# Attention then a mixture of experts on one core: smaller first row transfers, first v rows in float32, a later start of GpSimd's queue and a scripted opening

## The chip, the cores and the metric

The kernel runs on one core of one Trainium2 chip. The metric is the device time of one execution in microseconds; the number before the change is the median of three runs, 360.63 us (360.43 to 360.79). A core has five engines that run on their own and meet through semaphores: TensorE (PE, matrix products and transposes), VectorE (DVE), ScalarE (ACT), GpSimd (POOL) and SyncE (SP). Transfers between the large memory and the core's own memory are issued by an engine's queue: here by SP and ACT (plain copies and transposes) and by POOL (copies that also change float32 into bfloat16). All are carried out by the same 16 DMA engines.

## What is computed

Attention with a sliding window of 128 rows and 4 sink rows, over 4 batches of 8 heads of 768 rows of 64, and then a mixture of 4 experts over the 3072 rows of 512 that come out of it:

```python
scores = scale * q @ k.T                      # per batch and head
keep = (pos[None, :] < 4) | ((rel >= 0) & (rel < 128))
a = softmax(where(keep, scores, -1e9))
x = concat_heads(a @ v)                       # 3072 x 512
p = domain_probs / (domain_probs.sum(-1) + 1e-9)
out = sum over e of p[:, e] * (relu(x @ w1[e]) @ w2[e])   # w1: 512 x 1024, w2: 1024 x 512
```

Everything that comes in and goes out is float32; the products are done in bfloat16.

## The kernel before

**Tiles and stages.** A batch has three groups g of 256 rows, and its heads come in four pairs hp of two heads (2 x 64 = 128 columns). For batch 0 a pair of a group goes through five steps. "flip" (`transposes`) turns q and k rows on TensorE into qkT. "todo" is `scores`: the products sps, and exponentials on ScalarE into aT. For group 0 of batch 0 the mask is added beforehand as a product of ident with the tile low (L698); else VectorE multiplies by mask0 or mask1. "values" forms od from aT and vx (a tile of v rows with a column of ones), and divides by that column: reciprocal R and a product on VectorE into onat. "turn" transposes onat into xT on TensorE, copied out by ScalarE or VectorE. For groups 1 and 2 there are sink terms too: `sink_keys` and `sink_values`, computed on GpSimd for batch 0 from the rows vsf.

**Experts.** `Mixture` takes xT through the first layer (hps, L1098, into H) and the second (acc, L1425) for the first two groups of batch 0; w1 and w2 are an expert's weights. The other groups, and for some experts the first two also, use a scheme with seven half-size products (cps, L1181; acc, L1350) in place of eight, which needs sums of weight blocks ("forms", L402 to L408 and L367 to L373) and of xT blocks (token differences T, made by `tokens`, L1150), all on VectorE.

**What sets the order.** The program is straight-line code written out by a planner that runs while the kernel is built. It keeps an estimated clock per engine in the dictionary t ("sw" is GpSimd's transfer stream, "hw" the other), calls `later` to put off work of VectorE and ScalarE with a time from which it is ready and a slack, and in a loop at the end picks the next step of TensorE among those that are ready: attention (`Attention.options`), first-layer units, second-layer products. Constants such as TOKEN0, GATE0, MARGIN, GROW or STEP0 are its slacks, thresholds and priorities. While nothing is ready early in the run it puts in dummy products (`idle_products`, L572), and it starts with nine of them.

**The opening.** `load_first` (L285) loads the first 256 q and k rows of batch 0 in float32 as two halves of four heads: q on the sync queue, k on ScalarE's queue, 256 KB each. `cast_first` (L306) turns a half into bfloat16, q on VectorE and k on ScalarE. The sync queue then loads the routing table dp (L455), eight strips of sink rows vsf (L500) and the probabilities pr (L503). GpSimd's queue loads, in this order (L519 to L529): v 0 and 1, the rows tb 2 and 3 (q and k of group 1), v 2, the first quarter of w1 of expert 0, v 3, the other three quarters, w2 of expert 0. Later loads follow from the list `loads` (L1464). The gate rows (`gates_by_row`, L459) are normalised and stored once the planner's clock is past GROW.

Of the kernel before, what the change touches and what calls it, by code (L numbers as in the profile page):

```python
# [16 lines left out]
def kernel(  # L17
# [42 lines left out]
    NGATE = 5  # L60
    START = {0: (1, 0), 1: (0, 1), 2: (0, 0), 3: (0, 0)}
# [9 lines left out]
    EARLY = 0.138  # L71
    GATE = 5742
    GATE0 = 5043
    FORM = 19230
    FORM2 = 38137
    TOKEN0 = 220
# [4 lines left out]
    MARGIN = 828  # L81
    FULL = 8
    STEP0 = 0.155
    READY = 39
# [7 lines left out]
    GROW = 22996  # L92
# [16 lines left out]
    FLIP = 179  # L109
# [175 lines left out]
    def load_first():  # L285

        raw = {name: mo.tile([P, 2, 4, 2 * D], FP32, name=f"{name}raw", tag=f"wide{i}", bufs=1) for i, name in enumerate("qk")}
        for half in range(2):
            hs = slice(4 * half, 4 * half + 4)
            for name, src in (("q", q), ("k", k)):  # L290
                x = raw[name][:, half]
                (nc.sync if name == "q" else nc.scalar).dma_start(
                    out=x, in_=src[0, hs, 0:G, :].rearrange("h (p t) d -> p h (t d)", t=2),
                )
                nat[0, half, name, "raw"] = x
            landed["first", half] = ((4870.0, 5180.0), (7550.0, 7350.0))[half]
            t["sp"] += 530

# [7 lines left out]
    def cast_first(half):  # L306
        hs = slice(4 * half, 4 * half + 4)

        def cast(at):
            cast_at[half] = at  # L310

        part = join(2, cast)
        for i, name in enumerate("qk"):
            def run(engine, i=i, name=name):
                copy(
                    engine, first[name][:, :, hs, :],
                    nat[0, half, name, "raw"].rearrange("p h (t d) -> p t h d", t=2),
                )
                part(clock(engine, 512))
            later(("dve", "act")[i], landed["first", half][i], 0, run)  # L320
# [126 lines left out]
    load_first()  # L447
# [88 lines left out]
    low = [lent[:, 5 * P:8 * P], lent[:, 8 * P:10 * P]]  # L536
    nc.vector.tensor_scalar(
        out=low[0].rearrange("p (n q) -> p n q", n=3)[:, 0::2], in0=two, scalar1=LOW, scalar2=-LOW, op0=ALU.mult, op1=ALU.add,
    )
    nc.vector.tensor_scalar(out=low[0][:, P:2 * P], in0=own, scalar1=-LOW, scalar2=None, op0=ALU.mult)  # L540
    nc.vector.memset(low[0][0:NSINK, 0:2 * P], 0.0)
# [4 lines left out]
    t["dve"] = t["act"] = 4600.0  # L546
    cast_first(0)
    flush(4700.0)
    for x in vx:
        nc.vector.memset(x[:, :, D:DX], 1.0)  # L550
    t["dve"] += 240.0
# [5 lines left out]
    nc.vector.memset(half, 0.0)  # L557
    for ph in range(2):
        nc.vector.memset(half[64 * ph:64 * ph + 64, ph:ph + 1], 1.0)
    for x in ksd:  # L560
        nc.vector.memset(x, 0.0)
    for x, y in zip((mask0, mask1), low):
        nc.vector.tensor_scalar(out=x, in0=y, scalar1=1 / LOW, scalar2=1.0, op0=ALU.mult, op1=ALU.add)
    t["dve"] += 400.0
    cast_first(1)
# [13 lines left out]
    def transposes(b, g, hp):  # L579
# [3 lines left out]
        ready = max(cast_at[hp // 2] if (b, g) == (0, 0) else rows_at(b, g), free_at(2 if (b, g) == (0, 0) else 1))  # L583
        slots, trs = [], []
        for i in range(2 if (b, g) == (0, 0) else 1):
            slots.append(pick())
            trs.append(bank(slots[i], [P, 2, 2, P], BF16, "tr"))
            ring[slots[i]] = 1e12
        hs = slice(2 * hp, 2 * hp + 2)
# [17 lines left out]
        if (b, g) == (0, 0):  # L607
            part = join(2, copied)
            for i, engine in enumerate(("dve", "act")):
# [75 lines left out]
    def scores(b, hp, g, more=False):  # L685
# [10 lines left out]
        if biased:  # L696
            for ph in range(2):
                nc.tensor.matmul(sps[ph][:, 0:w], lhsT=ident, rhs=low[min(g, 1)], start=True, stop=False, skip_group_check=True)  # L698
# [62 lines left out]
    def values(b, hp, g):  # L761
# [47 lines left out]
        def run(engine):  # L809
# [3 lines left out]
            if b < ONACT:  # L813
# [47 lines left out]
    class Attention:  # L861
# [24 lines left out]
        def flip_ready(self):  # L886
            _, b, g, hp = self.flips[0]
            rows = cast_at.get(hp // 2, 1e12) if (b, g) == (0, 0) else rows_at(b, g)
            return max(rows, free_at(2 if (b, g) == (0, 0) else 1), scored_at.get(b - 1, 0.0))

        def options(self):

# [72 lines left out]
    class Mixture:  # L965
# [164 lines left out]
        def tokens(self):  # L1130
# [9 lines left out]
            if at > t["pe"]:  # L1140
                return
# [314 lines left out]
    idle_products(acc[1], 9)  # L1456
# [140 lines left out]
```

## Time and profile before

| | |
|---|---|
| median of three runs | 360.63 us (360.43 to 360.79) |
| profiled execution | 360.94 us |
| its span | 359.2 us |
| PE busy | 349.9 us (97%), 4678 matrix instructions |
| DVE busy | 309.0 us (86%), 703 instructions |
| ACT busy | 168.6 us (47%), 430 instructions |
| POOL busy | 68.9 us (19%), 90 instructions |
| q0, transfers of GpSimd's queue | 17.31 MB, 53.3% of 16 engines' span |
| q1, transfers of the sync queue | 19.32 MB, 29.9% |
| q10, transfers of ScalarE's queue | 0.52 MB, 0.6% |

The span goes from the first to the last event that the profiler shows; what the profiled execution took beyond it lies around it. In a line of the time line the columns are start, duration (both us), engine, line of the kernel, operation, tiles, shapes, number of instructions merged, and in brackets the idle time of the engine before it and what ended that. PEld is a weight load of TensorE; SPq, ACTq are issues of those queues. In the line of forty digits each digit is the busy share, in tenths, of a fortieth of the span (9.0 us). A matrix instruction's duration includes its way through the array, so instructions that follow each other overlap, and the pace of a group of them is the better measure.

### The profile page before, as it was taken

The numbers are of one execution on the slowest core, as the hardware profiler recorded it, in microseconds if no ns is written. First come the engines' busy times: TensorE is split into PE (matmuls) and PEld (weight loads), VectorE is DVE, ScalarE is ACT, GpSimd is POOL, SyncE is SP. The second block draws the span as 40 slices with busy tenths as digits, with TensorE's granted clock in tenths as the row PEclk, the third lists the DMA queues.
The fourth block names the chain that finished last, engine by engine and source line by source line (L and its number), as shares of the span: only waits on it lengthen the run. The fifth ranks groups of instructions, "written<-read, shape, count | busy, mean of one in ns | idle before, by whom it ended". The sixth has DMA issues, their size and how long they took to land.

```text
span 359.2 us, 11107 instructions
## 1 busy us (share of the span) xinstructions
PE 349.9 (97%) x4678; PEld 302.7 (84%) x4678; DVE 309.0 (86%) x703; ACT 168.6 (47%) x430; POOL 68.9 (19%) x90
## 2 busy tenths in 40 slices
PE   8899999999999999999999999999999999999995
PEld 3575687777588998998998998899899999999884
DVE  6779889998799799899699799799789899989630
ACT  5856341437883824556444732943752722222110
POOL 8934115211270531020030530000000000000000
PEclk9999999999999999999999999999999999999999
DMA  9999999999994999675077999131042211100011
GB/s 176 186 194 204 222 212 174 145 125 150 202 151 53 151 174 131 75 98 67 31 62 119 151 133 158 47 71 32 20 66 58 59 44 64 31 31 31 1 60 59
DMA packets 115318, 37.86 MB, mean 105 GB/s; under 512 B 97196, under 2 KB 110764, under 8 KB 115268
## 3 DMA queue, kind: packets, MB, share of 16 engines
q0 software_dynamic: 74416, 17.31, 53.3%
q1 hardware_dynamic: 39796, 19.32, 29.9%
q8 instruction: 36, 0.59, 0.7%
q10 hardware_dynamic: 1056, 0.52, 0.6%
q14 instruction: 14, 0.11, 0.1%
HBM read 41.03 MB, written 6.34 MB: 132 GB/s over the span
## 4 chain that ended last, share of the span: by engine, by line
PE 86%; DMA 6%; ACT 3%; DVE 2%; issue 1%; POOL 1%; SPq 0%; ACTq 0%; DVEq 0%
PE cps L1181 38%; PE acc L1350 34%; PE acc L1425 6%; DMA vx<-in_v_dram 3%; PE sps L704 2%; PE od L784 2%; PE hps L1098 2%; DMA kraw<-in_k_dram 2%; DMA scratch<-in_moe_domain_probs_dram 1%; ACT onat L823 1%; ACT aT L744 1%; PE od L777 1%; DVE aT L752 0%; DVE onat L814 0%; DVE osb L1435 0%
## 5 line engine op out<-in xcount | busy, mean ns | idle before, releaser
L1181 PEld LDWEIGHTS <-w 128*128 128x128 bf16 x1408 | 86.3, 98 | 3.2 <-issue 0.8
L1350 PEld LDWEIGHTS <-H 128*128 128x128 bf16 x720 | 66.4, 98 | 8.0 <-issue 1.6
L1215 DVE SCALAR_TENSOR_TENSOR H<-cps,gates 128x512 bf16<-128x512 f32 x105 | 69.6, 684 | 0.0
L1350 PE MATMUL acc<-w,H 128*128 128x256 bf16 x432 | 57.5, 273 | 0.5 <-ACT acc L1379 0.5
L1181 PE MATMUL cps<-T,w 128*128 128x128 bf16 x704 | 52.5, 219 | 0.5 <-DVE cps L1231 0.5
L1181 PE MATMUL cps<-xT,w 128*128 128x128 bf16 x704 | 52.0, 219 | 0.0
L744 ACT ACTIVATE aT<-sps 128x512 bf16<-128x512 f32 (+1 forms) x96 | 46.3, 573 | 3.5 <-PE sps L704 3.4
L1224 ACT COPY cps<-cps 128x512 f32<-128x512 f32 x44 | 25.4, 586 | 46.1 <-PE cps L1181 36.8
L1397 ACT COPY osb<-acc 128x256 f32<-128x256 f32 x40 | 15.2, 379 | 56.9 <-PE acc L1350 49.2
L823 ACT ACTIVATE onat<-od,R 128x64 bf16<-128x64 f32 x144 | 33.1, 352 | 17.8 <-DVE R L811 17.8
L1350 PE MATMUL acc<-wf,H 128*128 128x256 bf16 x288 | 39.2, 273 | 0.0
L1181 PEld LDWEIGHTS <-qkn 128*128 128x128 bf16 x576 | 35.1, 98 | 1.3
L1231 DVE TENSOR_TENSOR cps<-H,cps 128x512 f32<-128x512 f32 x40 | 27.7, 692 | 8.9 <-PE cps L1181 5.3
L1350 PEld LDWEIGHTS <-S 128*128 128x128 bf16 x320 | 30.2, 98 | 4.8 <-issue 1.4
L329 POOL DMA_DIRECT2D vx<-in_v_dram x24 | 21.4, 902 | 62.2 <-PE od L784 50.5
L1237 ACT COPY H<-cps 128x512 f32<-128x512 f32 x40 | 23.4, 593 | 19.3 <-PE cps L1181 19.2
L1425 PE MATMUL acc<-w,H 128*128 128x512 bf16 x128 | 30.1, 379 | 0.0
L1181 PEld LDWEIGHTS <-vf 128*128 128x128 bf16 x480 | 28.6, 98 | 0.3
L1246 DVE TENSOR_TENSOR H<-H,cps 128x512 f32<-128x512 f32 x40 | 27.0, 681 | 0.8 <-PE cps L1181 0.7
L1181 PE MATMUL cps<-T,qkn 128*128 128x128 bf16 x384 | 27.1, 219 | 0.0
L725 DVE TENSOR_TENSOR aT<-aT,mask 128x1024 bf16<-128x1024 bf16 (+1 forms) x36 | 23.1, 641 | 2.4 <-ACT aT L744 2.4
L1215 DVE SCALAR_TENSOR_TENSOR H<-H,gates 128x512 bf16<-128x512 f32 x35 | 23.9, 685 | 0.0
(125 smaller groups left out, 517.9 us busy)
## 6 DMA issues: line engine op xcount, KB each, us to landing
w<-in_moe_w_dram POOLq DMA_DIRECT2D x7, 1024.0 KB, 22.7
out_dram<-osb SPq DMA_DIRECT2D x23, 256.0 KB
gates<-gate_rows SPq DMA_DIRECT2D x40, 128.0 KB
vx<-in_v_dram POOLq DMA_DIRECT2D x24, 128.0 KB, 7.5
rows<-in_q_dram POOLq DMA_DIRECT2D x18, 128.0 KB, 7.0
rows<-in_k_dram POOLq DMA_DIRECT2D x18, 128.0 KB, 7.5
w<-in_moe_w_dram POOLq DMA_DIRECT2D x4, 256.0 KB, 8.8
kraw<-in_k_dram ACTq DMA_DIRECT2D x2, 256.0 KB
```

The costliest lines, as they stand in the source:

```text
L329: nc.gpsimd.dma_start(out=vx[tb][:, :, 0:D], in_=v[b, :, tb * P:(tb + 1) * P, :].rearrange("h p d -> p h d"),)
L725: nc.vector.tensor_mul(x, x, m[:, None, :].to_broadcast([P, n, 2 * w // n]))
L744: nc.scalar.activation(out=a[:, ph], in_=sps[ph][:, 0:w], func=AF.Exp, scale=scale)
L823: nc.scalar.mul(o[:, qi, hp, ph * D:(ph + 1) * D], od[:, qi, ph, 0:D], R[:, qi, ph])
L1181: nc.tensor.matmul(y[:, f], lhsT=A[:, d, f * P:(f + 1) * P], rhs=T[:, d], start=(m in ("P1", "P5") and f == 0 and d == 0), stop=(d == 1), ...
L1215: nc.vector.scalar_tensor_tensor(out=dst, in0=src, scalar=0.0, in1=gate, op0=ALU.max, op1=ALU.mult)
L1224: nc.scalar.copy(out=tiles["Y"], in_=y)
L1231: nc.vector.tensor_add(tiles["V"], c5, tiles["X"])
L1237: nc.scalar.copy(out=c5, in_=y)
L1246: nc.vector.tensor_add(c5, c5, y)
L1350: nc.tensor.matmul(x, lhsT=self.operand(b, g, e, m)[:, f], rhs=forms[e][m][:, f], start=(k == 0 and f == 0 and m in (("P1", "P5", "P2") if ...
L1425: nc.tensor.matmul(op, lhsT=H[:, fb // QF, fb % QF, s], rhs=w2_sb[e][:, fb, :], start=(fb == 0), stop=(fb == NFB - 1),)
```

## The change

- The first q and k rows come as four transfers each (one per head pair, 128 KB), k on ScalarE's queue, q on the sync queue, and are cast pair by pair; which engine casts and copies is set by the tuples KCAST and COPY0.
- v 0 and v 1 of batch 0 are loaded in float32 by the sync queue, behind q and ahead of the routing table, and cast by VectorE.
- GpSimd's queue starts with a copy of two elements of the third pair's raw k rows (HOLD0 = 3), and then loads in the order ORDER0: rows 2 and 3, two quarters of w1 of expert 0, v 2, v 3, the other two quarters, and w2.
- The first 16 attention steps of batch 0 follow SCRIPT0 (F flip, S scores, V values, T turn).
- The masks and clears of small tiles are put off on VectorE with a slack; the second mask tile low[1] and its two ScalarE activations go, and mask1 is made from own.
- In group 0 of batch 0 the pairs 1 and 3 are scaled on ScalarE (SCALE0).
- Token differences are not made before the planner's clock is at 28000 (TOKEN00), gate rows not before 30000 (GROW).
- Five dummy products at the start in place of nine (NIDLE), and other values for EARLY, GATE0, TOKEN0, MARGIN, STEP0, READY and FLIP.

```diff
+    SCRIPT0 = "FFSSFFSSVVTVTTTV"
+    FIRST = (3950.0, 4950.0, 5950.0, 6900.0)
+    KCAST = ("act", "act", "act", "dve")
+    COPY0 = (('any', 'act'), ('dve', 'act'), ('any', 'any'), ('dve', 'any'))
+    SCALE0 = (0, 1, 0, 1)
+    NTR = 2
+    NACT = 4
+    FIRSTV = (7300.0, 8600.0)
+    HOLD0 = 3
+    NIDLE = 5
+    CLEAR = 3000
+    ORDER0 = (10, 11, 0, 1, 6, 7, 2, 3)
-    EARLY = 0.138
+    EARLY = 0.109
-    GATE0 = 5043
+    GATE0 = 400
-    TOKEN0 = 220
+    TOKEN00 = 28000
+    TOKEN0 = 2000
-    MARGIN = 828
+    MARGIN = 2000
-    STEP0 = 0.155
-    READY = 39
+    STEP0 = 0.215
+    READY = 100
-    GROW = 22996
+    GROW = 30000
-    FLIP = 179
+    FLIP = 400
...
     def load_first():
-        raw = {name: mo.tile([P, 2, 4, 2 * D], FP32, name=f"{name}raw", tag=f"wide{i}", bufs=1) for i, name in enumerate("qk")}
-        for half in range(2):
-            hs = slice(4 * half, 4 * half + 4)
+        raw = {name: mo.tile([P, H, 2 * D], FP32, name=f"{name}raw", tag=f"wide{i}", bufs=1) for i, name in enumerate("qk")}
+        vraw = mo.tile([P, 2, H, D], FP32, name="vraw", tag="osb", bufs=1)
+        for hp in range(NHP):
+            hs = slice(2 * hp, 2 * hp + 2)
             for name, src in (("q", q), ("k", k)):
-                x = raw[name][:, half]
-                (nc.sync if name == "q" else nc.scalar).dma_start(
+                x = raw[name][:, hs]
+                (nc.scalar if name == "k" and hp < NACT else nc.sync).dma_start(
                     out=x, in_=src[0, hs, 0:G, :].rearrange("h (p t) d -> p h (t d)", t=2),
                 )
...
+        for tb in range(2):
+            nc.sync.dma_start(out=vraw[:, tb], in_=v[0, :, tb * P:(tb + 1) * P, :].rearrange("h p d -> p h d"))
+            t["sp"] += 530
+        return vraw
...
-    load_v(0, (0, 1))
-    t["sw"] += 500
-    for tb in (2, 3):
-        load_nat(0, tb)
-    load_v(0, (2,))
-    load_w1(0, 4, [0])
-    load_v(0, (3,))
-    for i in range(1, 4):
-        load_w1(0, 4, [i])
+    if HOLD0:
+        nc.gpsimd.tensor_copy(out=held, in_=raw[HOLD0 - 1])
+        t["pool"], t["sw"] = FIRST[(HOLD0 - 1)] + 300.0, 8000.0
+    for x in ORDER0:
+        if x < 4:
+            load_w1(0, 4, [x])
+        elif x < 8:
+            load_v(0, (x - 4,))
+        else:
+            load_nat(0, x - 8)
...
-    nc.scalar.activation(out=low[1][:, 0:P], in_=own, func=AF.Copy, scale=-LOW)
-    nc.scalar.activation(out=low[1][:, P:2 * P], in_=own, func=AF.Copy, scale=LOW, bias=-LOW)
...
+    for tb in range(2):
+        def cast_v(engine, tb=tb):
+            copy(engine, vx[tb][:, :, 0:D], vraw[:, tb])
+            landed["v", 0, tb] = clock(engine, 512)
+        later("dve", FIRSTV[tb], 200, cast_v)
...
-            if b < ONACT:
+            if b < ONACT and not (g == 0 and SCALE0[hp]):
...
         def options(self):
+
+            if not self.b and self.steps < len(SCRIPT0):
+                step = {"F": "flip", "S": "todo", "V": "values", "T": "turn"}[SCRIPT0[self.steps]]
+                mine = [x for x in self.choices() if x[1] == step]
+                if mine:
+                    yield from mine
+                    return
+            yield from self.choices()
...
-            if at > t["pe"]:
+            if at > t["pe"] or t["pe"] < TOKEN00:
                 return
...
-    idle_products(acc[1], 9)
+    idle_products(acc[1], NIDLE)
```

More of the change, by code (lines that the diff above doesn't have):

```diff
@@ L316, in run @@
                     engine, first[name][:, :, hs, :],
-                    nat[0, half, name, "raw"].rearrange("p h (t d) -> p t h d", t=2),
+                    nat[0, hp, name, "raw"].rearrange("p h (t d) -> p t h d", t=2),
                 )
-                part(clock(engine, 512))
-            later(("dve", "act")[i], landed["first", half][i], 0, run)
+                part(clock(engine, 256))
+            later(("dve", KCAST[hp])[i], landed["first", hp][i], 0, run)
     def rows_at(b, g):
@@ L445 @@
     forms_at = {}
-    load_first()
+    vraw = load_first()
+    raw = [nat[0, hp, "k", "raw"][:, 0, 0:2] for hp in range(NHP)]
     NT = Ntok // P
@@ L588, in transposes @@
             ring[slots[i]] = 1e12
+        trs = (trs * 2)[:2]
         hs = slice(2 * hp, 2 * hp + 2)
@@ L608, in transposes @@
             part = join(2, copied)
-            for i, engine in enumerate(("dve", "act")):
+            for i, engine in enumerate(COPY0[hp]):
                 def run(engine, i=i):
```

60 lines of the change are left out of this document (33 added, 27 removed).

## The prediction

> **What bounds the kernel now.** I read the page first, then the time line and the table of windows of the first 47 us, then the waits of the sync queue and the transfers by window.
>
> ```profile
> span 359.2 us, 11107 instructions
> PE   8899999999999999999999999999999999999995
> DMA  9999999999994999675077999131042211100011
> PE 86%; DMA 6%; ACT 3%; DVE 2%; issue 1%; POOL 1%; SPq 0%; ACTq 0%; DVEq 0%
> ```
>
> TensorE bounds it, and the DMA engines are full for the first 13 slices (117 us) as well. "Busy" flatters TensorE, since it counts dummy products and pipelining; so I count real work by its pace: 8 products of L1181 take 0.447 us, 4 of L1350 take 0.437, 8 of L1425 1.73, 8 of L1098 0.87. By that count the real work of the first 26.7 us is about 14.4 us and 12.3 are lost; from 26.7 to 47 about 1.3 of 20.3 are lost, and from 47 to 355.5 about 7 of 308. The change works where the 12.3 are.
>
> ```profile
> 2.28 1.95 POOL L329 DMA_DIRECT2D vx<-in_v_dram  x2
> 4.94 0.62 ACT L300 CAST qkn<-kraw 128x512 bf16<-128x512 f32 x1 [1.19 <-DMA kraw<-in_k_dram]
> 5.41 0.71 PE L593 MATMUL tr<-ident,qkn 128*128 128x128 bf16 x8
> 11.39 0.87 ACT L744 ACTIVATE aT<-sps 128x384 bf16<-128x384 f32 x2 [0.33 <-PE sps L704]
> 13.88 0.38 ACT L300 COPY xT<-tx 128x256 bf16<-128x256 bf16 x1
> 15.04 1.05 PE L1098 MATMUL hps<-xT,w 128*128 128x256 bf16 x8
> 16.81 0.27 PE L665 MATMUL sinks<-qkT,ksd 128*32 128x256 bf16 x1 [0.39 <-DVE qkT L300]
> 25.52 0.90 POOL L352 DMA_DIRECT2D w<-in_moe_w_dram  x1 [5.04 <-DMA w<-in_moe_w_dram]
> 26.70 1.90 PE L1425 MATMUL acc<-w,H 128*128 128x512 bf16 x8
> ```
>
> The reader is to see a chain: first real product at 5.41, last xT of group 0 at 14.26, first expert product at 15.04, first second-layer product at 26.70. The line at 25.52 dates w2 of expert 0: GpSimd was released by its landing, near 25. Two things set the pace: a chain through ScalarE and VectorE until some 23 us, and the software queue's stream of weights.
>
> ```profile
> SPq L500 <- DMA kraw<-in_k_dram: 3.0, 2, 1.5
> q10 hardware_dynamic: 440, 0.22, 92.4%
> q1 hardware_dynamic: 104, 0.06, 25.1%
> q0 software_dynamic: 66, 0.01, 13.2%
> ```
>
> The three queue lines are of 5 to 6 us: q0, GpSimd's queue, begins only as the first rows drain, though GpSimd issued at 2.28. Between 6 and 8 it moves 0.29 MB, which is the two v tiles. The sync engine stood twice for 1.5 us, each time until k rows landed: after q, k, q, k, the routing table and three sink rows, eight transfers, the next one waited.
>
> **Smaller first transfers.** The rows move at 0.33 and 0.32 MB/us (3 to 5 us). The first half pair is 0.52 MB, its k cast starts at 4.94; a pair's q and k are 0.26 MB, so 0.8 us less: 4.1. ScalarE now issues four transfers at 0.5 us (end 2.9), then the table load (1.28), so it is free at 4.2. A cast of half the columns is bounded by 0.31 and 0.62; I take 0.35. Transposes then start near 4.7, 0.7 sooner. The last rows still land near 7.0, as now (second k cast 7.03): bytes and pace are the same.
>
> **The fixed order** puts all four scores ahead of the values. ScalarE's work for group 0: three casts (1.05), some four copies (0.38 each, 1.5), eight exponentials (two in 0.87, 3.5), in all 6.1 from 4.2, with 0.3 for gaps 10.6, against 12.26 now. From there to the last xT it is 2.0 us now; pair 3 is scaled on ScalarE (four of L823 at 0.205, 0.82, against 0.42), so 13.0 against 14.26: **1.3 gained**. If each step waits for the other engines as now, only the 0.7 stays; bounds 0.7 and 1.7. The two mask activations that fall away (0.6) were hidden under the wait for k; so were the nine dummy products of which four go.
>
> That last edit could leave the array cold. The dummies start 0.43 us apart and only after 4.26 does the spacing fall to 0.15 or less, while the PEclk row says full speed throughout. The Trainium skill (TensorE: Matmul & The Clock Gate, Part 1) says that the array runs at half rate until a window of about 3.4 us was busy; the spacing agrees, about 2.9 us after the start at 1.40. The planner still fills waits above 220 ns with short dummies, so I charge nothing; cold, the 16 transposes and 8 bias products of group 0 would cost 16 x 0.055 + 8 x 0.16 = 2.2 us, mostly beside ScalarE.
>
> **v on the sync queue.** v 0 is the ninth transfer and waits for the first rows (4.1), then v follows the rows at once: 0.52 MB in 1.6 to 1.9 us, data 6.0 to 7.9, landed near 8.8 with the 0.9 that k takes from its last packets (6.0) to its cast (7.03). Two casts of 512 columns on VectorE (0.70 to 0.87 each) end by 9.6; the first values now wait for v until 9.30 anyway and come later in the new order. VectorE has 2.1 idle us of 6 between 4 and 10, which hides the 1.6. Routing table, sink rows and probabilities are behind v on the sync queue and slip some 2 us; sink values are read at 13.81, the rest after 22: hidden, with 3 us in hand for the sink rows.
>
> **GpSimd's queue.** It waits for the third k rows (6.1) and a tiny copy; first issue near 6.35. What is behind that wait: all later software loads, and the sink keys (13.17 now). From first issue to first packet it was 3.4 us at the start (2.28 to 5.7) and 1.5 later (142.79 to 144.3). First packets thus at 7.85 to 9.75; today the same stream, q and k rows of group 1, comes after v, at 8.0. The stream is moved by -0.15 to +1.75. I take **+0.6**, since the slow start overlapped with rows draining until 6. The skill (DMA: Bandwidth & Descriptors, Latency and other measured facts) gives about 1 us to the first byte of this path; by it the stream would open at 7.35, under v's tail, and the sum would be 0.6 better. The order inside it changes less: w1's first part comes after two loads rather than five, landing near 13.3 instead of 14.5, and v 2 and 3 (needed at 18.5) near 16.6. Two of GpSimd's issues (0.98 each) go.
>
> **VectorE's work moved.** Eight token differences (0.28 each, 2.3) leave 14.2 to 24.9 and the gate rows (1.05) leave 22.8, all to 28 us and later. That takes away the 0.39 at L665 and some 0.7 us around it, which keeps the gain above alive through group 1. But between 28 and 45 VectorE is busy 15.0 of 17 us, and between 47 and 84 36.2 of 37:
>
> ```profile
> 28.00:30.00 2.00, 2.00 (x33) 1.48 (x33) 1.97 (x4) 0.49 (x1) 1.76 (x2) 1.00 1.40 201
> 55.00:60.00 5.00, 5.00 (x36) 3.34 (x35) 5.00 (x9) 0.00 (x0) 1.75 (x3) 1.00 2.14 165
> ```
>
> (Third column from the sum on is VectorE.) 3.35 into 2.0 of room leaves 1.35 over. If VectorE runs ahead with the start, none is paid; I take 0.4 of 0 to 1.35. Other planner constants (margin, bias of choices, a slack of L1128) reorder later work; the waits of TensorE at 84 to 104 are 1.5 us, so I bound this by -1.5 and +1.5 and take 0.
>
> **Sum.** w2 of expert 0 lands at 25.5. By then TensorE can have done all that is done at 26.70 plus the product group that ran at 28.44 (0.87): lead 1.2 + 0.7 (of 0.87) = **1.9**, bounds 0.85 (stream at +1.75) and 2.8 (stream early, chain end 24.75). Less 0.4 for w2 of expert 1, 0.6 later than now when TensorE comes 1.5 early, less 0.4 for VectorE: **1.1**. The profiled execution took 360.94 us (span 359.2 and 1.7 around it), so 359.8; the median of the runs shown is 0.3 lower: 360.63 - 1.1 = **359.5**.
>
> **Rivals.** (a) The lead is real and hidden. Work that needs no expert 2 ends at 60.1; expert 2's forms run at 53.9 to 58.9 and hang on weights that landed near 47.6. If stream and forms slip 0.6 and VectorE gives nothing, TensorE waits there, and the end is where it was: **360.6**. For it: DMA full; against: 1.2 us between forms and use. (b) VectorE becomes the bound, the slower side: the 1.35 left over and 0.3 of late stream push forms and evictions after 47, and the lead is used up: no lead, plus 1.0 to 1.35, **361.7**. It decides once VectorE is without idle time from 28 to 47 and token differences still wait at 40. For it: its 98% from 47 to 84, and TensorE's 0.50 wait for L1231 at 85.6; against: VectorE gets the lead too. (c) All goes well: stream at 7.85, lead 2.8 kept, part of the 1.5 us at 84 to 104 closed: **357.6**. (d) It doesn't do what it says: rows still land in one bunch at 5 and group 0 ends near 14; that is in (a).
>
> **Chances.** Forecast 0.41 (own range 358.6 to 360.2), (a) 0.17, (b) 0.27, (c) 0.15. A measurement of this kernel tells 0.2% (0.72 us) from no change. Faster: (c) and most of the forecast, 0.50; same 0.21; slower 0.29. The range takes in (c) and (b) but for their tails: 357.2 to 362.0.
>
> **What would show it.** First L593 near 4.7; last xT near 13; first software packets between 7.9 and 9.7; first L1425 near 25.6; VectorE's windows 28 to 47; whether the distance between the two kernels at L1425's last product (95.4 now) is that at 26. If first software packets come after 9.7, or group 0 ends no sooner than 14, or the lead at 26 is gone at 95, I am wrong in that step.

## The result and the profile after

The changed kernel takes 362.52 us (median of 4 runs, 362.02 to 363.12), the kernel before 360.61 beside it: a ratio of 1.0051 with an interval of 1.0039 to 1.0063. It is slower by 1.9 us where 1.1 less was forecast. The profiled execution took 362.14 us, with a span of 360.4. It is a quick one of its kernel, and that of the kernel before (360.94) a slower one, so the two traces are 1.2 us apart and show two thirds of the loss.

The page of the kernel after: its first line, the rows of the slices for TensorE and the DMA engines, and the shares of the chain that ended last.

```profile
span 360.4 us, 11122 instructions
PE   8998999999999999999999999999999999999995
DMA  8999999999996999465087999131041321000011
PE 81%; DVE 7%; DMA 7%; ACT 3%; issue 1%; POOL 0%; SPq 0%; DVEq 0%; POOLq 0%
```

The slices look alike. In the chain VectorE has risen from 2 to 7% and TensorE has fallen from 86 to 81%. That is the first hint: some stretch now ends on VectorE.

The time line of the kernel after, for the first 27 us (start, duration, engine, line, instruction; in brackets the idle time before it and what ended that):

```profile
4.79 0.63 PE L624 MATMUL tr<-ident,qkn 128*128 128x128 bf16 x4
...
5.93 0.18 POOL L539 CAST held<-kraw 128x2 bf16<-128x2 f32 x1 [3.41 <-DMA kraw<-in_k_dram]
6.05 1.04 POOL L272 DMA_DIRECT2D qkn<-in_q_dram  x1
6.07 0.54 PE L729 MATMUL sps<-lent,ident 128*128 128x384 bf16 x2
...
7.25 0.34 PE L735 MATMUL sps<-qkT 64*128 64x256 bf16 x4
...
7.93 0.43 DVE L318 CAST vx<-vraw 128x512 bf16<-128x512 f32 x1 [0.56 <-DMA vraw<-in_v_dram]
8.27 0.42 DVE L318 COPY qkT<-tr 128x256 bf16<-128x256 bf16 x1
9.01 0.71 DVE L318 CAST vx<-vraw 128x512 bf16<-128x512 f32 x1 [0.32 <-DMA vraw<-in_v_dram]
9.64 0.40 DVE L318 COPY qkT<-tr 128x256 bf16<-128x256 bf16 x1
10.10 0.34 PE L735 MATMUL sps<-qkT 64*128 64x256 bf16 x4 [0.33 <-DVE qkT L318]
10.46 0.87 ACT L775 ACTIVATE aT<-sps 128x384 bf16<-128x384 f32 x2 [0.21 <-PE sps L735]
...
11.53 0.93 ACT L854 ACTIVATE onat<-od,R 128x64 bf16<-128x64 f32 x4 [0.20 <-DVE R L842]
12.78 0.65 ACT L318 COPY xT<-tx 128x256 bf16<-128x256 bf16 x2 [0.32 <-PE tx L876]
13.41 0.93 ACT L854 ACTIVATE onat<-od,R 128x64 bf16<-128x64 f32 x4
14.67 0.41 ACT L318 COPY xT<-tx 128x256 bf16<-128x256 bf16 x1
...
15.19 1.05 PE L1139 MATMUL hps<-xT,w 128*128 128x256 bf16 x8
...
26.50 0.88 POOL L370 DMA_DIRECT2D w<-in_moe_w_dram  x1 [4.99 <-DMA w<-in_moe_w_dram]
26.79 1.90 PE L1466 MATMUL acc<-w,H 128*128 128x512 bf16 x7
```

The first transposes are 0.62 us sooner (4.79 against 5.41), but the lead is gone at once. VectorE takes its work in order, and the two casts of v stand ahead of copies of qkT: each cast waits for v, each copy waits behind the cast, and TensorE starts the last scores of group 0 only at 10.10, 2.85 us after the second ones (7.25). From the end of the last exponential (11.33) it takes 3.75 us to the last xT at 15.08; before, it took 2.00 (12.26 to 14.26). In between ScalarE scales pair 1 (the row at 11.53) and pair 3 (13.41). The first expert product comes at 15.19 (15.04 before). The weights of expert 0's second layer, issued at 12.64, land 13.6 us later, at 26.2; before, issued at 10.87, they landed at 24.9. The rows at 26.50 and 25.52 are issues that waited for this. The first second-layer product starts at 26.79 against 26.70.

The transfers by queue between 8 and 9 us (packets, MB, share of the 16 engines), first the kernel after, then the kernel before:

```profile
q0 software_dynamic: 283, 0.07, 96.0%
q1 hardware_dynamic: 75, 0.03, 16.7%
```

```profile
q0 software_dynamic: 727, 0.18, 181.3%
```

GpSimd issues at 6.05, packets come from about 8.0 on, and in their first microsecond they have less than half the pace of before (0.07 against 0.18 MB); from 9 to 10 us they have 0.17. So the stream behind the hold is 0.11 MB late, 0.6 us at that pace, and 1.3 us late where w2 of expert 0 lands.

The time line of VectorE in the kernel after, where it masks the attention weights aT (L783) for the products of group 2:

```profile
32.97 0.28 DVE L1191 TENSOR_TENSOR T<-xT 128x256 bf16<-128x256 bf16 x1
33.17 0.42 DVE L783 TENSOR_TENSOR aT<-aT,mask 128x512 bf16<-128x512 bf16 x1
33.51 0.28 DVE L1191 TENSOR_TENSOR T<-xT,T 128x256 bf16<-128x256 bf16 x1
33.71 0.42 DVE L783 TENSOR_TENSOR aT<-aT,mask 128x512 bf16<-128x512 bf16 x1
34.04 0.29 DVE L1191 TENSOR_TENSOR T<-xT,T 128x256 bf16<-128x256 bf16 x1
...
34.58 0.69 DVE L424 TENSOR_TENSOR vf<-w,vf 128x1024 bf16<-128x1024 bf16 x1
35.18 0.42 DVE L783 TENSOR_TENSOR aT<-aT,mask 128x512 bf16<-128x512 bf16 x1
```

The waits in the same stretch (us in total, times, longest), and the windows of all engines from 32 to 36 us (window, its length, then PE, PEld, DVE, ACT, POOL):

```profile
PE od L815 <- DVE aT L783: 0.7, 1, 0.7
```

```profile
32.00:36.00 4.00, 3.30 (x43) 1.86 (x43) 3.96 (x12) 3.88 (x9) 0.56 (x1) 1.00 1.16 208
```

The moved token differences (L1191) lie between the masks, which ran one behind the other in the kernel before (four from 31.69 on). VectorE is busy 3.96 of 4 us, and TensorE waits 0.70 us for the mask at 35.18. The third second-layer group starts at 35.91 against 34.92. From here on the distance stays: first product of L1222 at 48.00 against 46.94, last product at 355.97 against 354.85, span 360.4 against 359.2. In this execution the kernel has used up its lead of 0.6 us by 27 us, and loses 1.0 more between 31.5 and 36.

### The profile page after: what moved, and what is told of

Read it like the earlier page. It is cut to its first block, busy times and chain, and to the rows that moved or that the text cites. A ratio compares the mean times of both kernels' runs of the same rounds, so it can differ in the third digit from the quotient of the medians.

```text
span 360.4 us, 11122 instructions
## 1 busy us (share of the span) xinstructions
PE 350.6 (97%) x4672; PEld 303.8 (84%) x4681; DVE 306.6 (85%) x703; ACT 171.4 (48%) x441; POOL 67.3 (19%) x89
## 4 chain that ended last, share of the span: by engine, by line
PE 81%; DVE 7%; DMA 7%; ACT 3%; issue 1%; POOL 0%; SPq 0%; DVEq 0%; POOLq 0%
PE cps L1222 35%; PE acc L1391 33%; PE acc L1466 5%; DMA qkn<-in_k_dram 3%; PE sps L735 2%; PE od L815 2%; PE hps L1139 2%; DVE H L1256 2%; DMA vsf<-in_v_dram 1%; DMA vraw<-in_v_dram 1%; ACT onat L854 1%; DVE H L1287 1%; DMA kraw<-in_k_dram 1%; ACT aT L775 1%; PE od L808 1%
## 5 line engine op out<-in xcount | busy, mean ns | idle before, releaser
L1222 PEld LDWEIGHTS <-w 128*128 128x128 bf16 x1408 | 86.5, 98 | 3.3 <-issue 0.8
L1222 PE MATMUL cps<-T,w 128*128 128x128 bf16 x704 | 52.7, 219 | 0.3 <-DVE H L1287 0.2
L1222 PE MATMUL cps<-xT,w 128*128 128x128 bf16 x704 | 52.4, 219 | 0.0
L854 ACT ACTIVATE onat<-od,R 128x64 bf16<-128x64 f32 x152 | 34.9, 346 | 16.7 <-DVE R L842 16.7
L1222 PEld LDWEIGHTS <-qkn 128*128 128x128 bf16 x576 | 35.1, 98 | 1.3 <-issue 0.2
L347 POOL DMA_DIRECT2D vx<-in_v_dram x22 | 19.4, 898 | 63.4 <-PE od L815 52.7
L1466 PE MATMUL acc<-w,H 128*128 128x512 bf16 x119 | 29.0, 379 | 0.4
L1222 PEld LDWEIGHTS <-vf 128*128 128x128 bf16 x480 | 28.6, 98 | 0.4
L1222 PE MATMUL cps<-T,qkn 128*128 128x128 bf16 x384 | 27.4, 219 | 0.1
```

What stands on the lines that cost most here:

```text
L347: nc.gpsimd.dma_start(out=vx[tb][:, :, 0:D], in_=v[b, :, tb * P:(tb + 1) * P, :].rearrange("h p d -> p h d"),)
L854: nc.scalar.mul(o[:, qi, hp, ph * D:(ph + 1) * D], od[:, qi, ph, 0:D], R[:, qi, ph])
L1222: nc.tensor.matmul(y[:, f], lhsT=A[:, d, f * P:(f + 1) * P], rhs=T[:, d], start=(m in ("P1", "P5") and f == 0 and d == 0), stop=(d == 1), ...
L1466: nc.tensor.matmul(op, lhsT=H[:, fb // QF, fb % QF, s], rhs=w2_sb[e][:, fb, :], start=(fb == 0), stop=(fb == NFB - 1),)
```

## The experiments

Each was timed beside the kernel before on the same chip. The median of that kernel was 360.6 to 360.8 us for e1 to e12, 361.08 for e13 to e16 and 360.89 for e17 and e18, so runs are compared by their ratios to it. Their intervals reach about 0.0012 to either side; two ratios closer than that are not told apart. They are not exactly the ratios of the medians.

**Moved VectorE work, and the late constants.** e1 puts the token differences back, e2 the gate rows, e4 the five constants that only concern later work; e3 makes the first two moves on the kernel before.

```diff
e1  -TOKEN00 = 28000       +TOKEN00 = 0
    -TOKEN0 = 2000         +TOKEN0 = 220
e2  -GROW = 30000          +GROW = 22996
e3  (kernel before)  TOKEN00 = 28000, TOKEN0 = 2000, GROW = 30000
e4  EARLY .138, GATE0 5043, MARGIN 828, STEP0 .155, FLIP 179
```

> The changed kernel with TOKEN00 = 0 and TOKEN0 = 220, so that the token differences L1191 are made when their xT is there (14 to 25 us) as before the change. Theory A (they now stand in VectorE's queue at 33 to 34.5 among the masks L783, and TensorE waits 0.7 us there for a mask): the wait at 34.7 to 35.7 goes, the fourth L1466 group starts near 34.9 instead of 35.9, time 361.5 instead of 362.5; if group 1 of attention then ends 0.7 later than 23.1, half of it is lost again, 362.0. Theory B (the loss comes from the later weight stream and from the late constants): no change within 0.3, 362.2 to 362.8.

> The changed kernel with GROW = 22996, so that the four gate-row operations (1.05 us of VectorE) run at 23 to 24 us where VectorE stands idle. Theory A: as VectorE is short of time at 31 to 36, the four operations that now run at 30.9 to 32.5 free 1.05 us there, the mask that TensorE waits for comes earlier and the whole 0.7 to 1.0 us returns: 361.5 to 361.8, with the fourth L1466 group near 35.0. If only the three token differences that run between masks do the harm, 362.3 to 362.6.

> The kernel before with the token differences held until 28000 (slack 2000) and GROW = 30000, and nothing else of the change. Theory A: the same 3.35 us land in VectorE at 28 to 36 and cost 0.7 to 1.0 us there; group 1 ends up to 0.7 us sooner but then waits for w2 of expert 0 (about 25.5): 361.0 to 361.6. Theory B: within 0.3 of the kernel before, 360.3 to 360.9.

> The changed kernel with EARLY, GATE0, MARGIN, STEP0 and FLIP as before the change (0.138, 5043, 828, 0.155, 179). The traces differ by 1.06 us at 61, by 0.7 at 96 and by 1.2 at the end, so these constants can have cost about 0.5 after 96 and gained 0.35 at 84: theory A gives 362.0 to 362.6 and the 1.0 at 35 stays; a rival by which the constants carry the loss gives 361.5 or less, with the fourth L1466 group near 34.9.

Measured: e1 362.39 us, 1.0044 (1.0032 to 1.0057); e2 362.80, 1.0060 (1.0048 to 1.0072); e3 361.08, 1.0008 (1.0000 to 1.0017); e4 362.75, 1.0055 (1.0042 to 1.0068). In e1 the 0.7 us wait is gone and the third group stands 8.5 us behind the first instead of 9.1, yet the time hardly falls. No single one of these edits is the cause: the moved work alone costs the kernel before 0.3 us, at the edge of what the interval tells from nothing, and the gate rows and the constants alone bring nothing back.

**The hold.** e5 takes the held copy away, e7 puts one into the kernel before, ahead of its v loads, and e12 lets it wait for the first k rows instead of the third.

```diff
e5  -        nc.gpsimd.tensor_copy(out=held, in_=raw[HOLD0 - 1])
    +        pass
e7  (kernel before)
    +    nc.gpsimd.tensor_copy(out=held, in_=nat[0, 0, "k", "raw"][:, 0, 0:2])
         load_v(0, (0, 1))
e12 -        nc.gpsimd.tensor_copy(out=held, in_=raw[HOLD0 - 1])
    +        nc.gpsimd.tensor_copy(out=held, in_=raw[0])
```

> The changed kernel without the copy that holds GpSimd's queue until the third k rows have landed; the plan and the order on every engine stay. Theory C (the late and slow opening of the software queue's stream is the loss: the first quarter of w1 lands near 15.2 to 16.3 and w2 of expert 0 at 26.4 to 28.0, against 14.5 and 25.5 before): the stream starts near 5.7 beside the v rows and w2 lands 0.7 to 1.5 sooner, at 25.5 to 26.5; first L1466 at 26.5 or sooner, time 361.0 to 361.6. Rival D (what counts is the 0.5 MB of float32 v on the same DMA engines, whenever GpSimd starts): the v casts end later than 9.7 and the stream is no earlier; 362.3 to 363.

> The kernel before with one thing of the change: GpSimd copies two elements of the first half of the raw k rows (landed at 4.9) ahead of its first load, so its queue opens 2.8 us later than 2.28; plan and order stay. Theory C: first packets come at 7.5 to 8.5 in place of 5.7, w2 of expert 0 lands 1.5 to 2.5 later than 25.5, first L1425 near 28, and the time is 361.8 to 362.8. If the queue starts quickly behind the drained rows (1.5 us after the issue, 6.6) the delay is 0.6 to 0.9 and the time 360.9 to 361.5. If the opening doesn't matter: 360.4 to 360.9.

> The changed kernel with GpSimd held by the first pair's raw k rows (landed near 4.1) instead of the third's (5.9 to 6.8); plan and order stay. The issues come some 2 us sooner, at 4.3. Theory C alone: w2 of expert 0 lands 1 sooner, time 361.3 to 361.9. Theory D (the software stream and the float32 v rows, 2048 pieces of 256 bytes, slow each other down, and VectorE stands in order behind the casts of v; without a hold v landed at 13.0 and 16.4 and the time was 369.8): first packets come at 5.8, in the middle of v, v lands after 10 and the time is 363 to 369.

Measured: e5 369.84 us, 1.0237 (1.0214 to 1.0261); e7 363.04, 1.0063 (1.0046 to 1.0081); e12 362.79, 1.0062 (1.0050 to 1.0074). The time line of e5:

```profile
13.03 0.43 DVE L318 CAST vx<-vraw 128x512 bf16<-128x512 f32 x1 [5.03 <-DMA vraw<-in_v_dram]
...
13.84 0.48 PE L729 MATMUL sps<-lent,ident 128*128 128x384 bf16 x1 [4.83 <-DVE qkT L318]
...
16.41 0.43 DVE L318 CAST vx<-vraw 128x512 bf16<-128x512 f32 x1 [2.62 <-DMA vraw<-in_v_dram]
```

Without the hold the software stream and the float32 v move at the same time, and v lands at 13 and 16.4 instead of 7.9 and 9.0. VectorE stands in the first cast for 5.03 us, and TensorE waits 4.83 us for the copy behind it. So the change needs its hold: float32 v on the sync queue and an open GpSimd queue don't go together. The Trainium skill (DMA: Bandwidth & Descriptors, Issuing engines are not separate DMA queues) says that transfers started by different engines run on the same 16 DMA engines and interleave; this trace agrees, with 0.24 MB of GpSimd's queue beside 0.13 MB of the sync queue between 10 and 12 us. For e5 neither expectation had a time near 369.84.

e7 shows the price of a hold without v on the other queue. Its time line:

```profile
5.41 1.92 POOL L329 DMA_DIRECT2D vx<-in_v_dram  x2
...
27.44 0.89 POOL L352 DMA_DIRECT2D w<-in_moe_w_dram  x1 [4.69 <-DMA w<-in_moe_w_dram]
...
29.18 1.90 PE L1425 MATMUL acc<-w,H 128*128 128x512 bf16 x8
```

An issue that comes 3.1 us later (5.41, not 2.28) moves the weights by 1.9 us and the start of the second layer by 2.5, and the time by 2.35. Part of that is v itself, which group 0 waits for there. It also shows that a loss in the first stretch is not absorbed later: of the 2.5 us 2.0 are there at the end (last product at 356.88 against 354.85), and e5, 8.2 us behind the changed kernel at that point, ends 7.7 behind it (last product at 363.66). In e12 GpSimd issues 2.3 us sooner than the changed kernel (3.78), but packets appear only with the last rows, at 7 to 8 us. Even so its stream is as early as in the kernel before:

```profile
25.29 0.89 POOL L370 DMA_DIRECT2D w<-in_moe_w_dram  x1 [2.03 <-DMA w<-in_moe_w_dram]
```

The weights that this row waits for land at 25.0 (24.9 before), and no product waits for weights ahead of that. Yet nothing is gained, contrary to both expectations: the casts are still in the way, the last scores start at 10.60, and the last xT comes at 15.59. An early stream alone isn't enough.

**The fixed order, and v back on GpSimd's queue.** e8 lets the planner choose group 0's order; e6 loads v by GpSimd ahead of the other loads and has no hold.

```diff
e8  -SCRIPT0 = "FFSSFFSSVVTVTTTV"
    +SCRIPT0 = ""
e6  -HOLD0 = 3                              +HOLD0 = 0
    -ORDER0 = (10, 11, 0, 1, 6, 7, 2, 3)    +ORDER0 = (4, 5, 10, 11, 6, 0, 7, 1, 2, 3)
    (and load_first and the casts without vraw)
```

> The changed kernel with an empty SCRIPT0, so that the planner picks the first 16 steps itself. In the changed kernel the values of pairs 2 and 3 stand behind turns that wait for ScalarE and VectorE (L876, 0.6 and 0.4 us), and the last xT of group 0 is done at 15.1, against 14.3 before. Rival E: the last xT comes 0.5 to 0.8 sooner and the time falls by as much, to 361.7 to 362.0. Theory C: the first layer waits for w1 and w2 in either case, and the time stays, 362.3 to 362.8.

> The changed kernel with v 0 and 1 loaded by GpSimd's queue again, in the order of the kernel before (v 0, v 1, rows 2 and 3, v 2, first quarter of w1, v 3, the other quarters), no hold and no casts of v; the per-pair rows, the fixed order and the constants stay. Theory C: the stream is that of the kernel before (w2 at 25.5), so the first L1466 group is at 26.0 to 26.7 and only the 1.0 at 35 stays: 360.8 to 361.6. Rival E (the fixed order and the small transfers are what costs): 362 or more.

Measured: e8 362.94 us, 1.0057 (1.0043 to 1.0071), so the fixed order alone is not the cause. e6 369.91, 1.0245 (1.0218 to 1.0271), says nothing on the point: its edit also changed the planner's clocks, the planner wrote another order for the later work, and the loss lies there (the first second-layer product starts at 26.9, as with the change). The next runs keep every engine's order.

**The opening undone, order kept.** In e9 GpSimd loads v at 2.5 us, without hold, without v on the sync queue and without casts, while the planner is told the same times as in the changed kernel. e10 also puts the token differences back, e11 the gate rows and the five constants as well, which leaves the smaller first transfers and the fixed order.

```diff
-            nc.sync.dma_start(out=vraw[:, tb], in_=v[0, :, ...])
+            pass
...
-        nc.gpsimd.tensor_copy(out=held, in_=raw[HOLD0 - 1])
+        for tb in range(2): nc.gpsimd.dma_start(out=vx[tb][:, :, 0:D], in_=v[0, :, ...])
...
-            copy(engine, vx[tb][:, :, 0:D], vraw[:, tb])
+            pass
```

> The changed kernel, its plan and TensorE's order untouched, with the opening of GpSimd's queue undone: no hold, v 0 and 1 loaded by GpSimd ahead of its other loads, no float32 v on the sync queue and no casts of it. The other parts (per-pair rows, fixed order, moved VectorE work, constants) stay. Theory C (GpSimd's loads issued from 2.4 us on queue up behind the rows and start at full pace at 5.7; held loads lose that head start): w2 of expert 0 lands at 25.5 to 25.8 as before the change, instead of 26.4 to 28.1, the first L1466 group starts at 26.5 to 26.8 in every execution, and the time is 361.0 to 361.6 (the VectorE wait near 35 stays). Rival E (small transfers, order and constants): 362.2 or more.

> The run with the opening undone, and the token differences back at 14 to 25 us as well (TOKEN00 = 0, TOKEN0 = 220). Theory C with A: the stream is early, so the 0.9 that TensorE lost near 35 is now visible and returns: 360.3 to 360.8, level with the kernel before. If the VectorE work never mattered: as the run with the opening undone, within 0.2.

> Per-pair rows, fixed order and mask changes alone: the opening undone, token differences, gate rows and EARLY, GATE0, MARGIN, STEP0 and FLIP as before the change. If the earlier first product (4.8 against 5.4) is worth anything, 359.6 to 360.4; by theory C, which has the stream of weights set the pace from 26 us on, it is worth nothing: 360.4 to 361.0, with the first L1466 group at 26.3 to 26.8.

Measured: e9 361.69 us, 1.0023 (1.0013 to 1.0033); e10 360.49, 0.9995 (0.9986 to 1.0003); e11 360.19, 0.9985 (0.9977 to 0.9994). The token differences cost 1.2 us here (1.0 by the ratios), against 0.1 (0.3) with the hold. The time line of e11 shows what the change was to reach:

```profile
5.49 0.49 PE L729 MATMUL sps<-lent,ident 128*128 128x384 bf16 x2
...
6.61 0.34 PE L735 MATMUL sps<-qkT 64*128 64x256 bf16 x4
...
8.90 0.34 PE L735 MATMUL sps<-qkT 64*128 64x256 bf16 x4
...
14.34 1.92 PE L1139 MATMUL hps<-xT,w 128*128 128x256 bf16 x16
...
25.89 1.90 PE L1466 MATMUL acc<-w,H 128*128 128x512 bf16 x8
```

The last scores start 1.2 us sooner than in the changed kernel, the first expert product 0.85 and the second layer 0.9. But not all of that is the casts. This is the fastest of e11's twelve executions (359.26 us), and the openings of the profiled executions differ: with the same edit the last scores start at 9.85 in e9 and at 10.56 in e10, because the rows come later there (the third q rows are cast at 6.54 and 7.20, against 5.56 in e11 and 5.64 in the changed kernel). The time from the second scores to the last is freer of that. It is 2.29 to 2.33 us in e9, e10 and e11, 2.85 in the changed kernel, and 2.98 to 3.69 in the other runs with the fixed order that have a cast ahead of each copy (e1, e2, e4, e12, e18; e5 apart). So the casts hold up the last scores by 0.6 us in the changed kernel's trace and by up to 1.4 elsewhere. The other 0.6 stand before the second scores: eight transposes and two dummies take 1.28 us in the changed kernel (4.79 to the row at 6.07) and 0.70 in e11 (to 5.49).

**Casts or hold.** e13 leaves everything as in the changed kernel and only lets the two casts of v follow the copies of qkT on VectorE; e14 and e16 do this in e1 and with all of e1, e2 and e4. e15 is e9 with the held copy put back behind the v loads.

```diff
e13 later("dve", FIRSTV[tb], 200, cast_v)        # clock only
    later("dve", 9990.0 + tb, 0, cast_v_late)    # the cast itself
e15 +  nc.gpsimd.tensor_copy(out=held, in_=raw[HOLD0 - 1]) if tb else None
```

> The changed kernel with one thing moved: on VectorE the two casts of v stand behind the last two copies of qkT of group 0 instead of one ahead of each. Every engine's other order, every transfer and the hold stay. Theory C (the casts, each waiting 0.56 and 0.32 us for v and taking 0.43 and 0.71, hold up the copies that the last scores need): the last scores of group 0, at 10.10 us now, start near 9.4, the last turn near 13.7 instead of 14.39, and the time falls by 0.5 to 0.8 us, to 361.7 to 362.0. Theory O (the late opening of GpSimd's queue sets the pace): group 0 may end sooner, but the first-layer products or the second layer wait for weights as much longer, and the time stays at 362.3 to 362.8.

> The same, and the token differences back at their old time. Theory C with the moved VectorE work as second cause: the gains add up as they did without the hold (0.83 and 1.2), 360.6 to 361.2. Theory O: as with the token differences back alone, 362.2 to 362.6.

> The kernel with the opening undone (v by GpSimd's queue at 2.5 us, no v casts, no v on the sync queue) and the hold put back, but behind v: only the later loads of GpSimd's queue wait for the third k rows. Theory C: the hold costs nothing while v fills the queue, and with no casts the time stays at 361.5 to 361.9, as without it. Theory O: the loads behind the hold come late, first-layer products wait for weights, 362.2 to 363.

> The changed kernel with the casts behind the copies, and the token differences, the gate rows and the five late constants as before the change: all of the opening with the hold, without its casts in the way and without the moved work. Theory C: 360.2 to 360.9, level with the kernel before or a little better. Theory O: 361.8 to 362.4.

Measured: e13 362.67 us, 1.0049 (1.0036 to 1.0062); e14 362.01, 1.0032 (1.0017 to 1.0046); e15 361.57, 1.0018 (1.0005 to 1.0031); e16 362.23, 1.0038 (1.0026 to 1.0050). The time line of e13:

```profile
9.72 0.34 PE L735 MATMUL sps<-qkT 64*128 64x256 bf16 x4
...
14.05 0.23 PE L876 MATMUL tx<-ident,onat 128*128 128x128 bf16 x1 [0.18 <-ACT onat L854]
...
15.15 1.05 PE L1139 MATMUL hps<-xT,w 128*128 128x256 bf16 x8 [0.24 <-DMA w<-in_moe_w_dram]
```

The casts did hold up the scores: these start 0.4 us sooner, 2.29 us after the second ones, and the last turn 0.3 sooner (14.05, not 14.39). But the first expert product starts where it was, since it now waits for its weights. In e16 such a wait is longer:

```profile
21.32 1.05 PE L1139 MATMUL hps<-xT,w 128*128 128x256 bf16 x8 [0.74 <-DMA w<-in_moe_w_dram]
```

First-layer products wait for weights, 0.2 to 1.5 us in sum, in eight of the ten traces with the hold and v on the sync queue (not in those of the changed kernel and e12), and in none of the kernel before, e3, e17, e9, e10 and e11. So neither theory stands alone: removing the casts shows the late stream, and an early stream (e12) shows the casts. e13 and e16 came out as theory O has it, e14 between the two. But e15, whose loads behind the hold come late too (it also waits 0.43 us for weights), was as fast as e9, within theory C's range. Theory O doesn't explain that, and it led to the end of the program.

**The end of the program.** The time line of the sync queue, the last store's issue, and the span of the core; the kernel after and its span are 357.00 and 360.4, those of the kernel before 355.89 and 359.2. First e9, then e17:

```profile
357.16 0.33 SPq L1383 DMA_DIRECT2D out_dram<-osb  x1
```

```profile
core 0: 359.8 us, clock 1.000
```

From the issue to the end of the span it is 2.64 us in e9, but 3.40 in the changed kernel and 3.31 in the kernel before. Over all runs it is 2.63 to 2.72 in e6, e9, e10, e11 and e15, which issue 111 transfers on the sync and ScalarE queues, and 3.31 to 3.47 in the others up to e16, which issue 113 (or 107, as the kernel before). In e9 the last TensorE product even starts 0.16 us later than with the change (356.13 against 355.97). So 0.7 of the 0.83 us that e9 had won may have nothing to do with the opening. In the traces these transfers use eight semaphores (the counters that tell when a transfer has landed) in turn, so their number decides on which of the eight the last store stands: it is number 108 in all runs with the short end, 103 in the kernel before and 99 in the changed kernel. e17 and e18 test it by splitting late loads of gate tiles, and move no other work.

```diff
+        n = 2 if len(gate_sb) >= 40 - 4 else 1      # e17, kernel before; e18: 40 - 6, changed kernel
+        for i in range(n):                          # halves of the same tile
-        nc.sync.dma_start(out=x..., in_=gate_rows[...])
+            nc.sync.dma_start(out=x...[half i], in_=gate_rows[... half i])
```

> The kernel before, with the last four of the 40 loads of the gate tiles split into halves: four more transfers on the sync queue, 111 instead of 107 on the sync and ScalarE queues together, nothing else moved on any engine. Theory T (the end of the program depends on which of the eight places of transfers in flight the last store stands on): from the last store's issue to the end of the span 2.6 to 2.75 us instead of 3.31, and the time falls by 0.6 to 0.7 us against the kernel before, ratio 0.998. Rival R (the shorter end of the runs with the opening undone comes from v going by GpSimd's queue): the end stays at 3.3 to 3.4 and the time within 0.2 us of the kernel before.

> The changed kernel, with the last six loads of the gate tiles split into halves: 119 transfers instead of 113, nothing else moved. Theory T: the last store stands on the same place as with 111; from its issue to the end 2.6 to 2.75 us instead of 3.40, and the time falls by 0.7 us, to some 361.8, as much as undoing the opening brought. Rival R: the end stays at 3.4 and the time at 362.4 to 362.8.

```profile
356.17 0.33 SPq L1342 DMA_DIRECT2D out_dram<-osb  x1
```

```profile
core 0: 358.9 us, clock 1.000
```

Measured: e17 360.15 us, 0.9975 (0.9965 to 0.9985), 2.73 us from the last issue to the end; e18 361.99, 1.0030 (1.0019 to 1.0041), 2.67 us. Four small transfers more make the kernel before faster by 0.74 us, and six bring the changed kernel from 1.0051 to 1.0030, 0.76 us. The split itself isn't what shortens the end, since e9, e10, e11 and e15 split nothing. So the number of transfers sets 0.7 us of the end. e17 has the lowest ratio of this study, below both kernels; e11's is not told from it.

If the end is apart from the rest, as e17 and e18 suggest, e9, e10, e11 and e15 can be compared with the rest when 0.7 us (0.0019) is put on them: opening undone 1.0042, tokens back alone 1.0044, both 1.0014, and with gate rows and constants 1.0004, against 1.0051. Each of the two alone brings some 0.3 us, which the intervals don't tell from nothing; both together bring 1.3, and all 1.7. That is how two delays look that lie side by side: the late opening (hold, v and its casts) and VectorE's moved work. e15 becomes 1.0037, told neither from e9 nor from the changed kernel, so with the moved work in place it decides nothing on the hold. Within the opening e16 and e11 can be compared: they differ only in the hold and in v's way over the sync queue, with its casts already behind the copies, and 1.0038 against 1.0004 is 1.2 us. The place of the casts brings 0.4 between e1 and e14 (1.0044, 1.0032), which is not told from nothing. So most of the opening's share is the hold and v's way, not the place of the casts. And what is left of the change when both are gone, the smaller transfers and the fixed order, can't be told from the kernel before.

## Why the prediction was wrong

**What bounds the kernel.** The row of the DMA engines is full for twelve slices (108 us), not thirteen; no term of the sum rests on it.

**First rows at 4.7.** Right: 4.79. But this is the only part of the gain that arrived.

**Group 0's last xT at 13.0.** It came at 15.08, and most of this miss has nothing to do with v. The sum had the last exponential end at 10.6 and 2.4 us behind it: the 2.0 of the kernel before, and 0.4 for scaling pair 3 on ScalarE. In e11, which has neither casts nor hold, the exponentials end at 10.21, sooner than forecast, but 3.67 us follow; in the changed kernel they end at 11.33, and 3.75 follow. So 1.3 of the 2.1 is this stretch, which is 3.67 to 4.07 us in every profile with the fixed order but e5's, and 2.32 in e8 without it. With all scores first, ScalarE still has pair 1's scaling (0.93 at 11.53) behind its exponentials, and the turns wait for what it scales; the sum priced pair 3 alone. The last scores are 1.2 us later than in e11, 0.6 by the casts and 0.6 by the slower first products.

**Nothing charged for fewer dummies.** The first scores start at 6.54 in the changed kernel and at 5.91 in e11, since the first transposes run at about half the pace (1.28 us against 0.70), while the granted clock reads 1.000 in both. Both paces occur among kernels with five dummies (the slow one in e9, e10, e13 and e16 too, the quick one in e8), and with nine the first eight transposes take 0.71 us in the kernel before and 1.06 in e17. So the cost that was put at nothing is there in some executions; that the four dummies cause it is not shown.

**Casts hidden by 2.1 idle us of 6.** This step failed, by 0.6 us at the last scores. v landed as forecast (the second cast ended at 9.72, forecast 9.6), but idle time in sum says nothing about an engine that works in order. The two casts stood ahead of two copies, waited 0.56 and 0.32 us for v, and took the copies with them. The prediction named what is behind GpSimd's wait, but not what is behind VectorE's.

**Stream +0.6, and the lead of 1.9 us.** The stream was within its bounds but twice the size (first packets near 8.0, w2 of expert 0 at 26.2, which is 1.3 late). The step that carries the miss is the lead of 1.9 at the second layer: it was worked out as if only that last landing were delayed and TensorE came early to everything before. All that group 0 and 1 need between 13 and 25 us, the rows of group 1 and the pieces of the first layer, comes by the same stream. So TensorE waits for weights in most profiles with the hold, also where group 0 is sooner (e13, e16: 0.24 and 0.74 us). In the changed kernel's own profile there is no such wait, and group 0's end, 2.1 us later than forecast, has taken the lead already. Lead measured: -0.1 in that execution; in those of the other runs with the hold and v on the sync queue (e1, e2, e4, e8, e12, e13, e14, e16, e18) the second layer starts at 27.2 to 28.8, later than before.

**VectorE 0.4 of 0 to 1.35.** Mis-sized: 1.0 at 33 to 36 in the profiled execution, 1.2 between e9 and e10 (1.0 by the ratios). The condition of the text held, that none is paid if VectorE runs ahead with the start; it had no start to run ahead with.

**Late constants 0.** Right as a size: nothing by themselves (e4), 0.3 with the gate rows between e10 and e11, which is not told from nothing.

**Rivals.** The slower side, no lead and VectorE as the bound, at 361.7, came nearest, and its mechanism is half of what happened. It came sooner than its place (33 to 36 us, not after 47), and the late opening is the other half. The hidden lead falls: what the first 27 us lose is still lost at 355 (e5, e7), and in e11's profile a second layer that starts 0.8 sooner than before ends 1.0 sooner (last product at 353.83). The transfers did what they say, so the last rival falls too.

**Not in the sum.** The 0.7 us of the end were in no term. They cost the change only 0.09 (3.40 against 3.31), but they would have led the study to a wrong share for the opening.

Open: why the stream starts at under half pace after a late opening; how the 1.2 us between e16 and e11 divide between the hold and v's way over the sync queue; and why rows of the first group land so unevenly. The third q rows are cast at 5.56, 6.54 and 7.20 in e11, e9 and e10, which open alike, and between 5.64 and 6.51 in the changed kernel and the runs that open as it does.

## What to carry to other kernels

Work put into idle time of an in-order engine has to be placed between its neighbours, above all if it waits for a transfer: ask what stands behind it, not how much idle time there is in sum. When one stream feeds a whole stretch, a lead at its head is worth only what the stream leaves of it, and two delays side by side hide each other from experiments that undo one at a time, so undo both. Before crediting a saving to a stage, look whether the last product came sooner: here 0.7 us were won or lost after it, by the number of transfers alone.

## What was unexpected of the hardware

The end of the program: from the last store's issue to the end of the span 2.63 to 2.73 us with 111 or 119 transfers on the sync and ScalarE queues, 3.31 to 3.47 with 107 or 113. That the count decides was shown (e17, e18), and with it changes the semaphore of the last store; by what the 0.7 us pass was not shown.

A software queue that opened late was slow at first. In the kernel before, with issues since 2.28, the two v tiles passed in 2 us (2104 packets, 0.29 MB from 6 to 8); in e7, which issues them at 5.41, 1984 packets and 0.25 MB took the 3 us from 7 to 10. In the changed kernel only the first microsecond was slow (283 packets from 8 to 9, then 670).
